# First loads in another order, conversion steps and a fourth of a convolution on GpSimd, and the last rests' y in a buffer of its own

## The chip, the cores and the metric

The kernel runs on one core of a Trainium2 chip. The metric is the device time of one execution in microseconds. TensorE (PE in the profile) multiplies matrices, VectorE (DVE), ScalarE (ACT) and GpSimd (POOL) work element by element, and SyncE (SP) issues every DMA of this kernel, in order. An instruction waits for others through semaphores, and each engine runs its own instructions in the order in which they stand.

## The reference, cut to what matters

```python
# 8 batches, 8 heads, 576 tokens, head_dim 64
kv  = einsum('bhsd,bhse->bhde', k, v)
out = einsum('bhsd,bhde->bhse', q, kv)
x   = out / sqrt(mean(out*out, -1) + 1e-6) * g_norm   # then [B, 576, 512]

gate_pre = sum(conv_w[j] * xp[:, j:j + 576, :] for j in range(5))   # xp: 4 zeros ahead
x = (sigmoid(gate_pre) * (x @ w_val)) @ w_out

h = gelu(x @ w_in); u, v = h[..., :512], h[..., 512:]
v = (v - mean(v)) / sqrt(var(v) + 1e-6) * g_ln
v = einsum('ts,bsd->btd', w_sg, v) + b_sg[None, :, None]
out = x + (u * v) @ w_out2
```

The weights w_val, conv_w, w_out, w_in and w_out2 come as 64-bit floats, the rest as 32-bit floats.

## The kernel before, in words

The work has two phases. Phase one takes the eight batches one after the other: attention (`kv`, then `o`, then a norm over each head, then a transpose `xT`), a convolution of five taps along the tokens for the gate, and two products (`val` with w_val, `y` with w_out). Its result `y_main` goes to DRAM; the last 64 tokens of four batches at a time are collected as "rests" and go to `y_rest`. Phase two reads both back and does the second block (`hv`, `hu`, `sg`, `out`).

A 32-bit product is made of three passes of TensorE: each factor is split into a high part h (rounded) and a low part l = value - h, and h*h, l*h and h*l are added up. For w_val and w_out the split starts from 64-bit floats. It is done in four pieces of 128 columns for each weight (`wv_pieces`, `wo_pieces`); `split` gives the steps of a piece, each on a tile of 128x512: ScalarE takes the magnitude (L117), VectorE does five steps (L127, L128, L120, L129, L124), ScalarE writes h (L162), and then come the last two steps, `a - h` (L167) and `l = (a - h) + c` (L169). In the kernel before, `first_weight` calls `split` with `on_pool` False: both last steps run on VectorE. `in_turn` interleaves the steps of the pieces that it is given.

The start of the program, up to the first batch's gate and the second weight's second piece, stands in a `manual_schedule` block: each engine runs these instructions in the order in which the code issues them. After that block a scheduler sets the order. Batch 0 is laid out there like this:

- the loads on SP; the conversions; `busy(n)` issues n small matmuls on a constant tile, whose result is not used, between the attention products;
- `kv_out` on ScalarE copies the attention's inner product into a block-diagonal tile `kvbd`, eight small copies, and `o` of the five token tiles reads it and Q;
- for each token tile, `square` (ScalarE), a sum (VectorE, L278), a power of -1/2 (GpSimd, L280), `scale` (VectorE, L283), a transpose (TensorE, L298), and the two parts of x (`X0h` on ScalarE, `X0l` on VectorE, L307);
- the gate: `taps` (ScalarE, L326) writes gate = tap 0 of each of the four channel blocks m, `conv` (VectorE, L332) adds taps 1 to 4 as one scalar_tensor_tensor of 128x576 for each block and tap, so 16 in all, and `sigmoid` (ScalarE) follows;
- TensorE meanwhile runs `val` of m = 0 and 1, the inner product `kv` of batch 1, and `val` of m = 2 and 3;
- `gated` (L360) multiplies each val block by its gate on VectorE, and `low` (L364) makes its low part. Only then come `o` and the norm of batch 1, whose transposes TensorE needs next.

TensorE's results stand in PSUM, in eight buffers that `bank` hands out in turn; a buffer is free again when the last reader of its earlier content is done. The scheduler has put the fifth `o` tile of batch 1 behind the VectorE read that frees a `val` buffer.

At the end, batch 7's `wout2` adds `out` to `res`, which holds `y_main`. The rests of batches 4 to 7 are added to another `res`, a tile of the same tag "Y", loaded from `y_rest` after the main part.

Of the kernel before, what the change touches and what calls it, by code (L numbers as in the profile page):

```python
# [21 lines left out]
NK = D // P  # L22
# [38 lines left out]
def body(ctx, tc, qT, k, v, gcol, w_val, conv_w, w_out, w_in, g_ln, w_sgT, b_sg, w_out2, out, out_r):  # L61
# [68 lines left out]

    def split(src, h, l, raw=None, tmp=None, k=None, on_pool=True):

# [23 lines left out]
        def steps():  # L156

            ops = st["steps"][1]
            yield ops[0]()
            yield ops[1]()  # L160
            a = ops[2]()
            act(h, flat(a), AF.Copy)  # L162
            yield
            yield ops[3]()
            c = ops[4]()
            yield
            (nc.gpsimd.tensor_tensor if on_pool else tt)(flat(a), flat(a), f32(h), op=ALU.subtract)  # L167
            yield
            tt(l, flat(a), flat(c), op=ALU.add)  # L169
            yield  # L170
# [48 lines left out]
    class Attention:  # L219
# [108 lines left out]
        def conv(self, ms):  # L328

            for j in range(1, KC):  # L330
                for m in ms:
                    stt(gate[:, m], x32[:, m, j:j + S], cw3[:, m, j:j + 1], gate[:, m], op0=ALU.mult, op1=ALU.add)  # L332

        def sigmoid(self, m):
# [296 lines left out]

    def first_weight(w, src, raws):
        return [split(src[:, m * P:(m + 1) * P], w[0][:, :, m * P:(m + 1) * P], w[1][:, :, m * P:(m + 1) * P],
                      raws[m], first[1][:, m % 2], NK, False)
                for m in range(NK)]

    wv_pieces = first_weight((wv[:, 0], wv[:, 1]), w_val, [first[0][:, i] for i in range(4)])
    wo_pieces = first_weight(wo, w_out, [spare[:, 0], spare[:, 1], first[0][:, 0], first[0][:, 1]])
    att = Attention(0)
# [17 lines left out]
    def in_turn(*pieces):  # L657

        for p in pieces:
            p[2]()  # L660
        running = [p[3]() for p in pieces]
# [4 lines left out]
    with tc.manual_schedule():  # L666
        for m in range(NK):
            wv_pieces[m][0]()
        wo_pieces[0][0]()
        att.load_kv()  # L670
        dma(gcol_s, gcol)
        dma(gln_s, g_ln)
        cw_work = taps()
        att.load_q()
        atts[1].load_kv()
        wo_pieces[1][0]()
        atts[1].load_q()
        in_turn(wv_pieces[0], wv_pieces[1])
        in_turn(wv_pieces[2], wv_pieces[3])
        wo_pieces[2][0]()  # L680
        wo_pieces[3][0]()
        busy(40)
        att.kv(0)
        busy(5)
        att.kv(1)
        busy(4)
        in_turn(wo_pieces[0])
        slots.drain()
        cw_work()
        steps = [att.o(t, None) for t in range(5)]  # L690
# [16 lines left out]
        moe = Moe(att.xh, att.xl, gate, y_main[0])  # L707
        steps[4][2]()
        for m in range(NK):
            att.taps(m)  # L710
        z = [moe.val(m, True) for m in (0, 1)]
        atts[1].kv(0)
        atts[1].kv(1)
        slots.drain()
        z += [moe.val(m, True) for m in (2, 3)]
        for a in (0, 2):
            att.conv((a, a + 1))
            att.sigmoid(a)
            att.sigmoid(a + 1)
        for m in range(NK):  # L720
            z[m][0]()
        for m in range(NK):
            z[m][1](False)
        in_turn(wo_pieces[1])
    marks = [latest()]
# [92 lines left out]
    for b in range(B):  # L818
# [23 lines left out]
        for m in range(NK):  # L842
            dma(res[:, m], y_main[b][:, m])
        if more:
            nrem = Rests((b + 1) // 2) if b % 2 else None
# [20 lines left out]
        if b % RG == RG - 1:  # L866
            res = sb("Y", [NK, RW])
            dma(res, y_rest[b // RG])
            for m in range(NK):
                wout2(m, ggr, res, out_r[b // RG])  # L870
                tick()
# [43 lines left out]
```

## Time and profile before

| what | value |
|---|---|
| time, median of 3 runs | 751.49 us (749.42 to 751.64) |
| the profiled execution: its own time, and its span | 752.53 us, 750.8 us |
| TensorE busy | 730.6 us, 97% of the span |
| VectorE busy | 589.0 us, 78% |
| ScalarE busy | 348.5 us, 46% |
| GpSimd busy | 152.1 us, 20% |

The span is the time from the first instruction to the last in the profiled execution; 1.73 us of its own time lie around it. A busy share is the part of the span in which the engine had an instruction in work. Shares of the whole say little about the first 100 us and the last 10, where the change is.

### The profile page before, as it was taken

The page shows a single profiled execution, that of the slowest core. Times are in us where ns is not written, and L with a number is a line of the kernel's source. Part 1 is how long each engine was busy: PE and PEld are TensorE (multiplying, and loading weights), DVE is VectorE, ACT ScalarE, POOL GpSimd, SP SyncE. Part 2 cuts the span into 40 slices and gives each one's busy share as a digit, 9 for nine tenths or more (in the row PEclk, how much of TensorE's full clock was granted, in tenths as well). Part 3 has the DMA queues.
Part 4 walks back from the last instruction along what each step waited for, and adds up shares of the span by engine and source line. Part 5 has one row for each costly group of instructions (what it writes and reads, how often), then busy time and mean ns, then how long its engine had stood idle before and what let it go on. Part 6 is the DMA issues. An engine that isn't in the chain of part 4 may idle for free.

```text
span 750.8 us, 11758 instructions
## 1 busy us (share of the span) xinstructions
PE 730.6 (97%) x4498; PEld 628.4 (84%) x4498; DVE 589.0 (78%) x1137; ACT 348.5 (46%) x662; POOL 152.1 (20%) x163
## 2 busy tenths in 40 slices
PE   7898999999899999999999999999999999999996
PEld 7787778778778787889989889888899888898896
DVE  6899979898779899889986786866866867867752
ACT  3657465565545756565543433434433424334320
POOL 0405437263344452221100010000100000100000
PEclk9899999999999999999999999999999999999999
DMA  9945243626144311344122211231330222111203
GB/s 284 337 138 190 86 161 134 202 87 211 56 131 158 107 69 71 106 156 142 58 70 85 71 57 56 71 99 42 99 127 10 75 85 63 64 57 43 99 1 112
DMA packets 56200, 80.15 MB, mean 107 GB/s; under 512 B 3664, under 2 KB 29264, under 8 KB 55120
## 3 DMA queue, kind: packets, MB, share of 16 engines
q1 hardware_dynamic: 56144, 79.40, 32.1%
q8 instruction: 35, 0.57, 0.3%
q14 instruction: 21, 0.17, 0.1%
HBM read 60.51 MB, written 18.87 MB: 106 GB/s over the span
## 4 chain that ended last, share of the span: by engine, by line
PE 82%; DVE 9%; DMA 3%; POOL 2%; issue 1%; ACT 1%; SPq 1%; DVEq 0%; POOLq 0%
PE sg L560 16%; PE hv L451 13%; PE out L201 12%; PE hu L201 12%; PE val L201 10%; PE y L201 9%; DVE G L332 5%; PE kv L252 3%; PE o L268 3%; PE xT L298 2%; POOL st L280 2%; PE hur L201 2%; DMA Q<-in_qT_dram 1%; DMA V<-in_v_dram 1%; DVE st L278 1%
## 5 line engine op out<-in xcount | busy, mean ns | idle before, releaser
L332 DVE SCALAR_TENSOR_TENSOR G<-X,cw,G 128x576 f32<-128x576 f32 x128 | 99.0, 819 | 6.4 <-ACT G L326 6.4
L201 PE MATMUL y<-Z,WOh 128*128 128x512 f32 (+1 forms) x320 | 100.5, 384 | 0.0
L463 POOL TENSOR_TENSOR bmv<-bmv,mhalf 128x1 f32<-128x1 f32 x36 | 21.5, 597 | 345.1 <-DVE bmv L462 345.1
L451 PE MATMUL hv<-wiv,X1h 128*128 128x512 f32 x256 | 83.3, 390 | 0.0
L201 PE MATMUL out<-Z,K 128*128 128x512 f32 x256 | 83.1, 389 | 0.0
L280 POOL TENSOR_TENSOR st<-st,mhalf 128x8 f32<-128x8 f32 (+1 forms) x40 | 74.2, 1862 | 27.4 <-DVE st L279 24.9
L201 PE MATMUL hu<-X1h,wiu 128*128 128x512 f32 x256 | 79.4, 391 | 0.0
L201 PEld LDWEIGHTS y<-Z,WOh 128*128 128x128 f32 x320 | 58.2, 189 | 11.3
L440 ACT ACTIVATE T<-T 128x512 f32<-128x512 f32 x68 | 42.9, 630 | 45.0 <-DVE T L437 44.8
L201 PE MATMUL y<-Z,WOl 128*128 128x512 f32 (+1 forms) x160 | 59.4, 373 | 0.0
L201 PEld LDWEIGHTS out<-Z,K 128*128 128x128 f32 x256 | 48.1, 188 | 10.0
L451 PEld LDWEIGHTS hv<-wiv,X1h 128*128 128x128 f32 x256 | 47.8, 188 | 9.8 <-ACT X1h L428 0.4
L201 PEld LDWEIGHTS hu<-X1h,wiu 128*128 128x128 f32 x256 | 46.6, 188 | 8.3
L561 DVE SCALAR_TENSOR_TENSOR T<-sg,gln,WOl 128x288 f32<-128x288 f32 x64 | 32.7, 516 | 26.5 <-PE sg L560 26.2
L201 PE MATMUL hu<-X1l,wiu 128*128 128x512 f32 x128 | 50.0, 391 | 0.0
L451 PE MATMUL hv<-wiv,X1l 128*128 128x512 f32 x128 | 49.9, 390 | 0.0
L201 PE MATMUL out<-Z,V 128*128 128x512 f32 x128 | 49.8, 389 | 0.0
L572 ACT ACTIVATE Z<-T 128x512 fp32r<-128x512 f32 x32 | 20.1, 631 | 58.1 <-DVE T L571 58.1
L268 PEld LDWEIGHTS o<-kvbd,Q 128*128 128x128 f32 (+1 forms) x320 | 41.0, 188 | 6.5 <-ACT kvbd L261 1.8
L268 PE MATMUL o<-kvbd,Q 128*128 128x128 f32 (+1 forms) x320 | 43.1, 283 | 1.6 <-DMA Q<-in_qT_dram 1.6
L201 PE MATMUL val<-X0h,WV 128*128 128x512 f32 x128 | 42.3, 412 | 0.0
L201 PE MATMUL val<-X1h,WV 128*128 128x512 f32 x128 | 41.3, 403 | 0.5 <-DVE T L360 0.5
(152 smaller groups left out, 1709.0 us busy)
## 6 DMA issues: line engine op xcount, KB each, us to landing
Q<-in_qT_dram SPq DMA_DIRECT2D x8, 1152.0 KB, 6.3
y_main<-Y SPq DMA_DIRECT2D x8, 1024.0 KB, 3.9
raw<-y_main SPq DMA_DIRECT2D x32, 256.0 KB, 3.1
Y<-y_main SPq DMA_DIRECT2D x32, 256.0 KB, 4.1
out_dram<-Y SPq DMA_DIRECT2D x32, 256.0 KB, 2.3
K<-in_k_dram SPq DMA_DIRECT2D x7, 1024.0 KB, 5.9
V<-in_v_dram SPq DMA_DIRECT2D x7, 1024.0 KB, 9.2
raw<-in_w_in_dram SPq DMA_DIRECT2D x16, 256.0 KB, 5.7
```

Of the source, the lines that this page charges most:

```text
L201: nc.tensor.matmul(ps, lhsT=a[:, kt, msl], rhs=x[:, kt], start=(i == 0), stop=(i == 3 * NK - 1))
L252: nc.tensor.matmul(self.pk[j][h, h], lhsT=self.k[:n, t, js][:, h], rhs=self.v[:n, t, js][:, h], start=(t == 0), stop=(t == 4))
L268: nc.tensor.matmul(po[:n, j * P:(j + 1) * P], lhsT=self.q[:, j, o:o + n], rhs=bd[:, j, :], start=True, stop=True)
L280: nc.gpsimd.tensor_tensor(st[:n, 2], st[:n, 1], mhalf[:n], op=ALU.pow)
L298: nc.tensor.transpose(pt[:, j * P:j * P + n], xo[:n, j * P:(j + 1) * P], ident[:n, :n])
L332: stt(gate[:, m], x32[:, m, j:j + S], cw3[:, m, j:j + 1], gate[:, m], op0=ALU.mult, op1=ALU.add)
L440: act(w, w, AF.Tanh, scale=CG * AG)
L451: nc.tensor.matmul(ps, lhsT=a[:, kt], rhs=p2["wiv"][:, w, kt], start=(i == 0), stop=(i == 3 * NK - 1))
L463: nc.gpsimd.tensor_tensor(mv[:, 3:4], mv[:, 2:3], mhalf[:, 0:1], op=ALU.pow)
L560: nc.tensor.matmul(ps, lhsT=a[:, msl], rhs=w, start=(n == 0), stop=(n == len(mm) - 1))
L561: later(0, lambda: stt(vs[:, sl], ps, gln_s[:, m:m + 1], p2["bsg"][:, sl], op0=ALU.mult, op1=ALU.add))
L572: act(g[:, 0], x, AF.Copy)
```

## The change

Four things change. (1) The order of the first loads, and how many dummy matmuls stand where: w_val's fourth piece is loaded after batch 0's k and v, and w_out's first piece after Q. (2) `on_pool` becomes a number: with 1 or 2 the step `a - h` runs on GpSimd, with 2 the last step too. w_val's four pieces and w_out's first two have 2, the others 1. Two more temporary tiles (in tag "Z") let the pieces run without sharing, and w_out's first two pieces are converted later: inside the first gate. (3) The gate of channel block 3 of batch 0 leaves `conv`: `conv_apart` lets ScalarE scale the shifted x and GpSimd add it to the gate, tap by tap. The low parts of `val` blocks 0 and 2 go to GpSimd too. (4) For the last batch, `y_rest` is loaded into the tag "XR", early, and not into "Y" at the end.

```diff
-    def split(src, h, l, raw=None, tmp=None, k=None, on_pool=True):
+    def split(src, h, l, raw=None, tmp=None, k=None, on_pool=1):
...
             (nc.gpsimd.tensor_tensor if on_pool else tt)(flat(a), flat(a), f32(h), op=ALU.subtract)
             yield
-            tt(l, flat(a), flat(c), op=ALU.add)
+            (nc.gpsimd.tensor_tensor if on_pool > 1 else tt)(l, flat(a), flat(c), op=ALU.add)
             yield
...
+        def conv_apart(self, m, x):
+
+            for j in range(1, KC):
+                act(x[:, j - 1], x32[:, m, j:j + S], AF.Copy, scale=cw3[:, m, j:j + 1])
+                nc.gpsimd.tensor_tensor(gate[:, m], gate[:, m], x[:, j - 1], op=ALU.add)
+
...
-    def first_weight(w, src, raws):
+    def first_weight(w, src, raws, tmps, on_pool):
         return [split(src[:, m * P:(m + 1) * P], w[0][:, :, m * P:(m + 1) * P], w[1][:, :, m * P:(m + 1) * P],
-                      raws[m], first[1][:, m % 2], NK, False)
+                      raws[m], tmps[m], NK, on_pool[m])
                 for m in range(NK)]
 
-    wv_pieces = first_weight((wv[:, 0], wv[:, 1]), w_val, [first[0][:, i] for i in range(4)])
-    wo_pieces = first_weight(wo, w_out, [spare[:, 0], spare[:, 1], first[0][:, 0], first[0][:, 1]])
+    more = sb("Z", [2, 3, D])
+    tmps = [t[:, i] for t in (first[1], more) for i in range(2)]
+    wv_pieces = first_weight((wv[:, 0], wv[:, 1]), w_val, [first[0][:, i] for i in range(4)], tmps, (2, 2, 2, 2))
+    wo_pieces = first_weight(wo, w_out, [spare[:, 0], spare[:, 1], first[0][:, 0], first[0][:, 1]],
+                             tmps[:2] * 2, (2, 2, 1, 1))
...
-        for m in range(NK):
+        for m in range(3):
             wv_pieces[m][0]()
-        wo_pieces[0][0]()
         att.load_kv()
         dma(gcol_s, gcol)
+        cw_work = taps()
+        wv_pieces[3][0]()
+        att.load_q()
+        wo_pieces[0][0]()
+        atts[1].load_kv()
         dma(gln_s, g_ln)
-        cw_work = taps()
-        att.load_q()
-        atts[1].load_kv()
         wo_pieces[1][0]()
         atts[1].load_q()
+        for m in range(3):
+            wv_pieces[m][2]()
         in_turn(wv_pieces[0], wv_pieces[1])
-        in_turn(wv_pieces[2], wv_pieces[3])
+        in_turn(wv_pieces[2])
+        cw_work()
+        wv_pieces[3][2]()
+        in_turn(wv_pieces[3])
         wo_pieces[2][0]()
         wo_pieces[3][0]()
-        busy(40)
+        busy(32)
         att.kv(0)
-        busy(5)
+        busy(12)
         att.kv(1)
-        busy(4)
-        in_turn(wo_pieces[0])
+        busy(20)
         slots.drain()
-        cw_work()
...
         steps[4][2]()
+        wo_pieces[0][2]()
         for m in range(NK):
             att.taps(m)
+        wo_pieces[1][2]()
+        in_turn(wo_pieces[0])
+        att.conv_apart(3, sb("Z", [KC - 1, S]))
         z = [moe.val(m, True) for m in (0, 1)]
...
-        for a in (0, 2):
-            att.conv((a, a + 1))
-            att.sigmoid(a)
-            att.sigmoid(a + 1)
+        att.conv((0, 1, 2))
+        for m in range(NK):
+            att.sigmoid(m)
+        in_turn(wo_pieces[1])
         for m in range(NK):
             z[m][0]()
         for m in range(NK):
-            z[m][1](False)
-        in_turn(wo_pieces[1])
+            z[m][1]()
...
+        if not more:
+            res_r = sb("XR", [NK, RW])
+            dma(res_r, y_rest[b // RG])
...
         if b % RG == RG - 1:
-            res = sb("Y", [NK, RW])
-            dma(res, y_rest[b // RG])
+            if more:
+                res_r = sb("Y", [NK, RW])
+                dma(res_r, y_rest[b // RG])
             for m in range(NK):
-                wout2(m, ggr, res, out_r[b // RG])
+                wout2(m, ggr, res_r, out_r[b // RG])
                 tick()
```

What this makes of each engine's row of instructions is shown at three places. The first is SP's first loads (`wiu` and `Y` hold the raw weights, `raw` the raw taps), before:

```order
L148 DMA wiu_88<-in_w_val_dram 128x4x256 x4
L148 DMA Y_90<-in_w_out_dram 128x4x256
L229 DMA K_102<-in_k_dram 128x2x512
L229 DMA V_103<-in_v_dram 128x2x512
L229 DMA K_102<-in_k_dram 128x2x512
L229 DMA V_103<-in_v_dram 128x2x512
L231 DMA K_102<-in_k_dram 64x512
L231 DMA V_103<-in_v_dram 64x512
L671 DMA gcol_76<-in_gcol_dram 128x1
L672 DMA gln_77<-in_g_ln_dram 128x4
L647 DMA raw_112<-in_conv_w_dram 128x40
L235 DMA Q_114<-in_qT_dram 128x4x576
```

and after the change:

```order
L150 DMA wiu_88<-in_w_val_dram 128x4x256 x3
L231 DMA K_101<-in_k_dram 128x2x512
L231 DMA V_102<-in_v_dram 128x2x512
L231 DMA K_101<-in_k_dram 128x2x512
L231 DMA V_102<-in_v_dram 128x2x512
L233 DMA K_101<-in_k_dram 64x512
L233 DMA V_102<-in_v_dram 64x512
L679 DMA gcol_76<-in_gcol_dram 128x1
L658 DMA raw_110<-in_conv_w_dram 128x40
L150 DMA wiu_88<-in_w_val_dram 128x4x256
L237 DMA Q_113<-in_qT_dram 128x4x576
L150 DMA Y_90<-in_w_out_dram 128x4x256
```

Half a megabyte of w_val and half a megabyte of w_out stood ahead of k and v; the first now stands behind them, the second behind Q.

The second is GpSimd from the end of its constants to the norm of batch 1, before (`st` with `mhalf` is the power, five for each batch):

```order
L207 MEMSET X_11_82 128x4x4
L280 TENSOR_TENSOR st_286<-st_286,mhalf_70 128x8
L280 TENSOR_TENSOR st_294<-st_294,mhalf_70 128x8
L280 TENSOR_TENSOR st_302<-st_302,mhalf_70 128x8
L280 TENSOR_TENSOR st_310<-st_310,mhalf_70 128x8
L280 TENSOR_TENSOR st_318<-st_318,mhalf_70 64x8
L279 TENSOR_SCALAR st_554<-st_554 128x8
L280 TENSOR_TENSOR st_554<-st_554,mhalf_70 128x8
```

and after the change, first the stretch up to the first power and then that from the last power of batch 0:

```order
L209 MEMSET X_11_82 128x4x4
L169 TENSOR_TENSOR wiv_89<-wiv_89,WV_79 128x512 x2
L171 TENSOR_TENSOR WV_79<-wiv_89 128x4x128 x2
L169 TENSOR_TENSOR Z_91<-Z_91,WV_79 128x512
L171 TENSOR_TENSOR WV_79<-Z_91 128x4x128
L169 TENSOR_TENSOR Z_91<-Z_91,WV_79 128x512
L171 TENSOR_TENSOR WV_79<-Z_91 128x4x128
L282 TENSOR_TENSOR st_293<-st_293,mhalf_70 128x8
```

```order
L282 TENSOR_TENSOR st_325<-st_325,mhalf_70 64x8
L169 TENSOR_TENSOR wiv_89<-wiv_89,WOh_80 128x512
L171 TENSOR_TENSOR WOl_81<-wiv_89 128x4x128
L340 TENSOR_TENSOR G_83<-G_83,Z_416 128x576 x4
L169 TENSOR_TENSOR wiv_89<-wiv_89,WOh_80 128x512
L171 TENSOR_TENSOR WOl_81<-wiv_89 128x4x128
L372 TENSOR_TENSOR Z_425<-T_439,Z_425 128x512
L281 TENSOR_SCALAR st_575<-st_575 128x8
L372 TENSOR_TENSOR Z_425<-T_510,Z_425 128x512
L281 TENSOR_SCALAR st_582<-st_582 128x8
L282 TENSOR_TENSOR st_575<-st_575,mhalf_70 128x8
```

Eight steps of w_val (names `WV`) now stand ahead of the first power, and w_out's four (`WOh`, `WOl`), the four additions of `conv_apart` (`G`) and two low parts of the gated val (`Z<-T,Z`) ahead of the first power of batch 1 (the last row).

The third is VectorE from the last low part of x, `X0l`, to the first gated val, `T<-val`, before:

```order
L307 SCALAR_TENSOR_TENSOR X0l_92<-xT_378,gcol_76,X0h_91 128x4x128
L332 SCALAR_TENSOR_TENSOR G_83<-X_11_82,cw_78,G_83 128x576 x4
L322 TENSOR_TENSOR XR_606<-X_11_82,XR_606 128x4x64
L332 SCALAR_TENSOR_TENSOR G_83<-X_11_82,cw_78,G_83 128x576 x12
L360 TENSOR_TENSOR T_413<-val_400,G_83 128x512
L360 TENSOR_TENSOR T_427<-val_414,G_83 128x512
```

and after the change:

```order
L309 SCALAR_TENSOR_TENSOR X0l_93<-xT_385,gcol_76,X0h_92 128x4x128
L127 TENSOR_SCALAR wiv_89<-Y_90 128x512
L128 TENSOR_SCALAR wiv_89<-wiv_89 128x512
L120 SCALAR_TENSOR_TENSOR wiv_89<-wiv_89 128x512
L129 TENSOR_SCALAR wiv_89<-wiv_89 128x512
L124 SCALAR_TENSOR_TENSOR wiv_89<-Y_90,wiv_89 128x512
L334 SCALAR_TENSOR_TENSOR G_83<-X_11_82,cw_78,G_83 128x576 x4
L324 TENSOR_TENSOR XR_627<-X_11_82,XR_627 128x4x64
L334 SCALAR_TENSOR_TENSOR G_83<-X_11_82,cw_78,G_83 128x576 x8
L127 TENSOR_SCALAR wiv_89<-Y_90 128x512
L128 TENSOR_SCALAR wiv_89<-wiv_89 128x512
L120 SCALAR_TENSOR_TENSOR wiv_89<-wiv_89 128x512
```

Four of the 16 conv steps are gone from VectorE, and the five steps of w_out's first piece stand ahead of the conv, those of its second piece behind it, with the first `T<-val` right after these.

## Rows read from the trace of the kernel before

**Rows 1.** Waits of TensorE (PE), 0 to 110 us; columns: us in total, times, longest

```profile
PE xT L298 <- DVE T L283: 3.2, 4, 1.2
...
PE val L201 <- DVE T L360: 0.5, 1, 0.5
```

**Rows 2.** TensorE's timeline, 2 to 30 us

```profile
2.27 11.23 PE L217 MATMUL warm<-ident 128*128 128x128 f32 x80 [2.27 <-POOL X L207]
...
23.45 6.55 PE L268 MATMUL o<-kvbd,Q 128*128 128x128 f32 x40 [1.57 <-DMA Q<-in_qT_dram]
```

**Rows 3.** Windows of 1 us on TensorE

```profile
22.00:23.00 1.00, 0.00 (x0) 0.50 0.95 344
27.00:28.00 1.00, 1.00 (x10) 0.98 1.05 401
```

**Rows 4.** VectorE's (DVE) timeline, 4 to 21 us

```profile
9.19 0.76 DVE L129 TENSOR_SCALAR wiv<-wiv 128x512 int32<-128x512 int32 x2
9.87 1.29 DVE L124 SCALAR_TENSOR_TENSOR wiv<-wiu,wiv 128x512 f32<-128x512 uint32 x2
11.07 1.28 DVE L167 TENSOR_TENSOR wiv<-wiv,WV 128x512 f32<-128x512 f32 x2
```

**Rows 5.** Groups of VectorE, 0 to 110 us; after the bars busy us and mean ns

```profile
L653 DVE TENSOR_TENSOR cw<-cv 128x20 f32<-128x20 f32 x1 | 0.2, 180 | 0.0
```

**Rows 6.** One line's instructions, all runs of it; min/median/max ns

```profile
L364 POOL TENSOR_TENSOR Z<-T,Z x18: 731/1298/1727, 96.1 to 330.2; 128x512 fp32r<-128x512 f32 x14, 128x256 fp32r<-128x256 f32 x4
```

**Rows 7.** The timeline of all engines, 303.9 to 305.6 us

```profile
303.71 1.35 POOL L364 TENSOR_TENSOR Z<-T,Z 128x512 fp32r<-128x512 f32 x1 [0.43 <-ACT Z L361]
...
304.42 1.25 DVE L332 SCALAR_TENSOR_TENSOR G<-X,cw,G 128x576 f32<-128x576 f32 x1
```

**Rows 8.** The timeline of all engines, 97.5 to 99.6 us

```profile
96.97 0.98 DVE L364 TENSOR_TENSOR Z<-T,Z 128x512 fp32r<-128x512 f32 x1
...
97.37 1.73 POOL L364 TENSOR_TENSOR Z<-T,Z 128x512 fp32r<-128x512 f32 x1
```

**Rows 9.** ScalarE's (ACT) timeline, 8 to 28 us

```profile
8.71 1.23 ACT L162 ACTIVATE WV<-wiv 128x512 fp32r<-128x512 f32 x2 [1.09 <-DVE wiv L120]
...
23.99 0.22 ACT L261 ACTIVATE kvbd<-kv 64x64 f32<-64x64 f32 x1
...
25.53 0.60 ACT L275 ACTIVATE T<-o 128x512 f32<-128x512 f32 x1 [1.08 <-PE o L268]
```

**Rows 10.** GpSimd's (POOL) timeline, 24 to 36 us

```profile
27.21 8.08 POOL L280 TENSOR_TENSOR st<-st,mhalf 128x8 f32<-128x8 f32 x5 [24.93 <-DVE st L279]
```

**Rows 11.** VectorE's timeline, 36.5 to 53.5 us

```profile
36.85 0.75 DVE L307 SCALAR_TENSOR_TENSOR X0l<-xT,gcol,X0h 128x512 fp32r<-128x512 f32 x1 [0.18 <-ACT X L303]
...
40.99 0.42 DVE L322 TENSOR_TENSOR XR<-X,XR 128x256 fp32r<-128x256 f32 x1
41.33 8.84 DVE L332 SCALAR_TENSOR_TENSOR G<-X,cw,G 128x576 f32<-128x576 f32 x12
50.08 1.88 DVE L360 TENSOR_TENSOR T<-val,G 128x512 f32<-128x512 f32 x3
52.46 0.69 DVE L360 TENSOR_TENSOR T<-val,G 128x512 f32<-128x512 f32 x1 [0.51 <-PE val L201]
```

**Rows 12.** The timeline of all engines, 56.6 to 61.2 us

```profile
56.68 3.62 PE L252 MATMUL kv<-V,K 128*64 128x64 f32 x79
...
57.28 1.64 POOL L280 TENSOR_TENSOR st<-st,mhalf 128x8 f32<-128x8 f32 x1
...
60.87 0.52 PE L298 MATMUL xT<-ident,T 128*128 128x128 f32 x3 [0.57 <-DVE T L283]
```

**Rows 13.** The timeline of all engines, from 744.5 us

```profile
744.39 0.28 PE L201 MATMUL out<-WOh,K 128*128 128x256 f32 x1
745.62 1.42 DVE L586 SCALAR_TENSOR_TENSOR Y<-out,Y 128x256 f32<-128x256 f32 x4 [5.90 <-DMA Y<-y_rest]
746.07 1.79 SPq L587 DMA_DIRECT2D out_dram<-Y  x4
```

More of the change, by code (lines that the diff above doesn't have):

```diff
@@ L657, in in_turn @@
     def in_turn(*pieces):
-        for p in pieces:
-            p[2]()
         running = [p[3]() for p in pieces]
```

## The prediction

> **What bounds the kernel now.** TensorE is the bound nearly everywhere, so I looked first for the places where it stands still, in its waits over the first 110 us. The reader is to see that little can be won there: four transposes of x wait 3.2 us in all for VectorE's scaled tiles, and one val product waits 0.5 us for a gated val of the batch before [rows 1]. Ahead of it stands the start: TensorE fills the time with 40 dummy matmuls (80 instructions, 0.281 us for two), then waits 1.57 us for Q, and the `o` products take 6.55 us [rows 2], because the granted clock is 0.50, which is 1.2 GHz, at 22 us, where TensorE has nothing to run, and back at 0.98 only in the microsecond from 27 [rows 3]. The end is the third place: the last matmul is over at 744.67, yet VectorE's last four additions start at 745.62, since the rests' y lands only then [rows 13].
>
> So the change can win at most the start, about 4 us of waits, and about 2 us of tail. What it can lose depends on what VectorE and GpSimd do to each other, which is the view I read longest.
>
> **Prices.** VectorE: a tensor_scalar of 128x512 0.34 us (two from 9.19 to 9.87), one with two inputs in SBUF 0.60 (two from 9.87 to 11.07) [rows 4]; so the five first steps of a piece 3 x 0.34 + 2 x 0.60 = 2.22, and the two last, which are moved, 1.20. A conv step 8.84 / 12 = 0.737, the step XR 0.34 [rows 11]. Six steps of the taps 6 x 0.18 = 1.1 [rows 5]. GpSimd: 1.30 for 128x512 with two inputs, 0.73 for 128x256 [rows 6]. It never ran 128x576 in this form; from the two widths 1.30 + 64 x 0.57 / 256 = 1.44, an estimate.
>
> A moved step thus takes twice as long, which would be free if GpSimd worked beside VectorE. The rows say it doesn't. A GpSimd operation ran from 303.71 to 305.06; the conv step that VectorE began at 304.42 took 1.25 us and ended at 305.67, 0.61 behind GpSimd's end [rows 7]. Turned round, VectorE's low part ended at 97.95, and the GpSimd operation that had begun at 97.37 took 1.73 us and ended at 99.10, 1.15 later [rows 8]. One waits for the other and then runs nearly its whole length: of 0.737 us 0.12 are saved, of 1.30 us 0.15, so 0.27 for each GpSimd operation set between two of VectorE's. Operations that read PSUM on VectorE were not held up.
>
> **The Trainium skill** says in "SBUF — State Buffer", section "Who interferes with whom", that a VectorE instruction with two SBUF inputs and a GpSimd instruction that reads SBUF exclude each other for a whole instruction. By the page alone, with nothing saved at a handover, the two sums below would each be 1.6 us longer and the forecast 757.4; the rows' 0.27 us is taken instead.
>
> **Step 1, the start.** At 9.33 (8.71 and half of 1.23) the first h is there [rows 9] and GpSimd wants to subtract; VectorE comes free at 9.87 [rows 4]. Until ScalarE can write the fourth piece's h, VectorE has to do two steps of the first pieces (1.20), the third piece (2.22), the taps (1.1) and three steps of the fourth (0.34 + 0.34 + 0.60 = 1.28): 5.8. GpSimd does six steps in turn with it: 7.8, less 6 x 0.27 = 1.6. That gives 9.87 + 5.8 + 7.8 - 1.6 = 21.9. Then h, 0.62, and the eight copies into kvbd, which ended at 24.21 before [rows 9] and take 1.8: 24.3. They stand behind this h on ScalarE, and TensorE's `o` waits for them. The loads are no later than that: half a megabyte less stands ahead of Q, which landed at about 23.4 [rows 2]. With 64 dummy matmuls instead of 49 TensorE has hardly stood still until then, so I take the full clock. The first `square` then comes at about 24.6, not 25.53, and the five powers, which follow one another (8.08 us for five [rows 10]), are **0.9 us earlier**. Ends: 1.6 earlier, if GpSimd takes nothing from VectorE and only the wait for Q of 1.57 [rows 2] goes; 0.7 later with no saving at handovers.
>
> **Step 2, the first gate.** I count on the clock of before and subtract 0.9 at the end. VectorE's last X0l ends at 37.60 [rows 11]. Until the conv's last step it then needs five steps of w_out's first piece (2.22), twelve conv steps (8.84) and XR (0.34); GpSimd, in turn with it, w_out's two last steps (2.60) and four additions (5.76). Six handovers save 1.6. 37.60 + 2.22 + 8.84 + 0.34 + 8.36 - 1.6 = 55.8, where the conv ended at 50.2 before [rows 11]. Who goes first hardly matters: the fourth gated val needs the last addition too. Then w_out's second piece, 2.22, stands in front of the first gated val: 58.0, not 50.08, and the fourth is done at 60.4, not 53.15 [rows 11]. TensorE has `kv` of the next batch to run until 60.3 [rows 12], but the fifth `o` tile ahead of it needs the PSUM buffer that the first gated val frees.
>
> Behind this VectorE sums the squares at once, since half of the low parts have gone. But GpSimd has four operations ahead of batch 1's first power: w_out's second piece and two low parts, 5.2 us from about 58.0, when ScalarE has written the piece's h, with half a microsecond of waits: 63.7, not 57.28 [rows 12], 6.4 later. Less the 0.9 of step 1, the first transpose of batch 1, which waited 0.57 us before [rows 12], comes 5.5 us later. The later powers find their sums ready; I take 1 us of it as made good over five tiles. TensorE is **4.5 us later**, step 1 in it. Bounds: if the additions find gaps, the three microseconds of transpose waits go away instead; without savings at handovers it is 3.3 more.
>
> **Step 3, later.** VectorE is rid of w_out's second piece (3.4) and two more steps (1.2) between 56 and 76 us, so the val wait [rows 1] goes: **0.5 less**. ScalarE's four more passes stand ahead of sigmoids that wait for VectorE's conv anyway; if the conv were done first, they would cost four times about 0.6. From there to the end TensorE is packed and keeps what it has.
>
> **Step 4, the tail.** TensorE's end plus 0.04 plus an addition of 0.42 gives 745.13 for the last addition instead of 747.04; the four issues no longer queue (1.79 us for four), and 2.94 us lie behind the last: 748.5 instead of 750.8, **2.3 less** (1.9 if the queueing stays) [rows 13]. The early load of half a megabyte follows four others on SP and waits for nothing that is late.
>
> **Step 5, the clock.** Between about 56 and 66 us TensorE now stands still twice for some microseconds. At the start it stood still in such a way, and its clock was at half for the five microseconds from 22 [rows 3]. Products at that speed cost up to 3 us; part is hidden in the waits. I take **1.0 more**, between 0 and 3.
>
> **Sum.** 4.5 - 0.5 - 2.3 + 1.0 = +2.7 us. The profiled execution took 752.53, which gives 755.2; it stood 1.0 above the median of the runs, 751.49, so I give 754.2.
>
> **Rivals.**
> - *GpSimd fits in beside VectorE* (the other side): its operations fall where VectorE reads PSUM or idles, or VectorE keeps its pace. For it speaks that VectorE stood waiting at the start and that ten microseconds of work leave it. Against it, rows 7 and 8, and a conv that leaves no gap from 38 to 50 us. Then step 1 gives 1.6, the transposes 3.2, the val 0.5, the tail 2.3: 7.6 less, 743.9; half of that, 747.7, if only the conv collides lightly. It decides at a first gated val at about 52 instead of 57.
> - *Mostly hidden* (no change): the same exclusion, but the powers run closer together and step 1 gives its full 1.6, so that TensorE is 1.8 us later and the tail and the val wait pay for it: 751.5 with half a microsecond for the clock. For it speaks that TensorE's transposes have y products between them; against it, that the first of them has none.
> - *Heavier*: nothing saved at handovers, or a clock that stays low for longer than at the start: 757 to 759.
>
> **Chances.** Forecast 0.35, heavier 0.12, mostly hidden 0.23, GpSimd beside VectorE 0.30. Within 0.3% (749.2 to 753.7, about what a measurement of this kernel tells from no change) fall the hidden case and a little of the forecast's lower end: 0.25. Faster 0.30, slower 0.45. The forecast's own range is 752 to 757; to hold eight in ten it must take in most of the fast case and the heavier one: 744.5 to 759.
>
> **What would show it.** In the profile of after: conv steps of 128x576 with a mean near 1.2 us instead of 0.81 while GpSimd adds to G; the first gated val near 57 and batch 1's first power near 63; TensorE waiting for the fifth `o` tile and the first transpose; the rests' additions at the end each following their matmuls within 0.1 us, with no load in front. The forecast is wrong if the conv steps keep 0.8 us and the transposes of batch 1 no longer wait; then the time is under 748.

## The result and the profile after

The changed kernel takes 756.68 us (median of 4 runs, 755.60 to 756.81), the kernel before 750.64 (4 runs): a ratio of 1.0076, with an interval of 1.0056 to 1.0095. It is slower by 6 us. The profiled execution shows only half of that, 755.6 beside 752.53, so a second execution of each kernel was profiled later (the last two experiments). Their landmarks stand side by side here, in microseconds from the start of each trace (starts, where no end is named; a transpose is that of one token tile):

| landmark | before, 1st | before, 2nd | after, 1st | after, 2nd |
|---|---|---|---|---|
| first `square` | 25.53 | 24.16 | 23.89 | 24.03 |
| last X0l ends | 37.60 | 35.96 | 35.61 | 35.74 |
| last conv step ends | 50.16 | 48.71 | 54.21 | 54.33 |
| first gated val | 50.08 | 48.63 | 56.71 | 56.83 |
| first power of batch 1 | 57.28 | 57.18 | 63.18 | 63.27 |
| first transpose of batch 1 | 60.87 | 60.77 | 66.92 | 67.01 |
| second transpose | 62.67 | 62.58 | 69.75 | 69.83 |
| first `y` product | 63.06 | 62.96 | 70.48 | 70.57 |
| third transpose | 65.93 | 65.83 | 74.32 | 75.43 |
| third block of `y` | 71.10 | 71.00 | 78.48 | 79.58 |
| first `hv` product | 318.66 | 318.71 | 324.19 | 326.89 |
| last matmul ends | 744.66 | 744.77 | 750.12 | 753.17 |
| span | 750.8 | 750.8 | 753.8 | 756.9 |
| own time | 752.53 | 752.56 | 755.60 | 758.64 |

First the waits of TensorE over the first 110 us (us in total, times, longest), which answer to [rows 1].

```profile
PE xT L300 <- ACT WOh L164: 5.0, 1, 5.0
PE o L270 <- DVE T L368: 3.5, 1, 3.5
PE xT L300 <- DVE T L285: 2.7, 2, 1.7
```

The val wait is gone, and two long stops have come: the fifth `o` tile waits 3.5 us for the first gated val, and the first transpose of batch 1 waits 5. The latter is put down to ScalarE's WOh, which ended at 66.84, but the scaled tile that the transpose reads was ready only at 66.78 (it starts at 66.10 and takes 0.68), so without ScalarE the wait would have been 0.1 shorter.

Next VectorE's timeline from 38 to 59 us, and GpSimd's from 40 to 70, which answer to [rows 11] and [rows 12].

```profile
38.24 4.04 DVE L334 SCALAR_TENSOR_TENSOR G<-X,cw,G 128x576 f32<-128x576 f32 x4
42.19 1.49 DVE L324 TENSOR_TENSOR XR<-X,XR 128x256 fp32r<-128x256 f32 x1
43.61 10.60 DVE L334 SCALAR_TENSOR_TENSOR G<-X,cw,G 128x576 f32<-128x576 f32 x8
54.13 0.41 DVE L127 TENSOR_SCALAR wiv<-Y 128x512 int32<-128x512 int32 x1
...
56.71 2.48 DVE L368 TENSOR_TENSOR T<-val,G 128x512 f32<-128x512 f32 x4
```

```profile
40.08 1.57 POOL L169 TENSOR_TENSOR wiv<-wiv,WOh 128x512 f32<-128x512 f32 x1 [6.50 <-ACT WOh L164]
41.73 1.68 POOL L171 TENSOR_TENSOR WOl<-wiv 128x512 fp32r<-128x512 f32 x1
43.36 7.31 POOL L340 TENSOR_TENSOR G<-G,Z 128x576 f32<-128x576 f32 x4
56.35 1.57 POOL L169 TENSOR_TENSOR wiv<-wiv,WOh 128x512 f32<-128x512 f32 x1 [5.68 <-ACT WOh L164]
58.00 1.29 POOL L171 TENSOR_TENSOR WOl<-wiv 128x512 fp32r<-128x512 f32 x1
59.25 1.29 POOL L372 TENSOR_TENSOR Z<-T,Z 128x512 fp32r<-128x512 f32 x1
60.62 0.52 POOL L281 TENSOR_SCALAR st<-st 128x8 f32<-128x8 f32 x1
61.22 1.27 POOL L372 TENSOR_TENSOR Z<-T,Z 128x512 fp32r<-128x512 f32 x1
62.58 0.52 POOL L281 TENSOR_SCALAR st<-st 128x8 f32<-128x8 f32 x1
63.18 1.71 POOL L282 TENSOR_TENSOR st<-st,mhalf 128x8 f32<-128x8 f32 x1
64.97 1.27 POOL L281 TENSOR_SCALAR st<-st 128x8 f32<-128x8 f32 x1
66.31 4.16 POOL L282 TENSOR_TENSOR st<-st,mhalf 128x8 f32<-128x8 f32 x2
```

From 40 to 51 us the two engines alternate strictly: twelve conv steps were left to VectorE, and with XR they took 15.97 us (38.24 to 54.21), where sixteen and XR took 12.09 before (38.07 to 50.16). The steps one by one, as the group of this tile gives them (min/median/max ns; first and last start):

```profile
L334 DVE SCALAR_TENSOR_TENSOR G<-X,cw,G x12: 805/810/1984, 38.2 to 53.4; 128x576 f32<-128x576 f32 x12
L340 POOL TENSOR_TENSOR G<-G,Z x4: 1591/1825/1830, 43.4 to 48.8; 128x576 f32<-128x576 f32 x4
```

The seven steps outside GpSimd's work took 0.81, the five beside it 1.85 to 1.98. Behind the conv come w_out's second piece, the gated vals, and then GpSimd's four operations, with the sums' small steps held up among them, before the first power at 63.18.

The tail, VectorE's last additions and the last matmul, answers to [rows 13]:

```profile
747.32 0.42 DVE L594 SCALAR_TENSOR_TENSOR XR<-out,XR 128x256 f32<-128x256 f32 x1 [0.99 <-PE out L203]
...
749.84 0.28 PE L203 MATMUL out<-WOh,K 128*128 128x256 f32 x1
750.15 0.42 DVE L594 SCALAR_TENSOR_TENSOR XR<-out,XR 128x256 f32<-128x256 f32 x1 [0.99 <-PE out L203]
```

Each addition follows its matmul, with no load in front. From the last matmul to the end of the span it is 3.7 us, where it was 6.1.

### The profile page after: what moved, and what is told of

It reads as the page before. It is cut to its first block, busy times and chain, and to the rows that moved or that the text cites. A ratio compares the mean times of both kernels' runs of the same rounds, so it can differ in the third digit from the quotient of the medians.

```text
span 753.8 us, 11833 instructions
## 1 busy us (share of the span) xinstructions
PE 732.5 (97%) x4528; PEld 630.2 (84%) x4528; DVE 592.0 (79%) x1117; ACT 350.8 (47%) x666; POOL 182.4 (24%) x183
## 4 chain that ended last, share of the span: by engine, by line
PE 86%; DVE 9%; POOL 3%; ACT 2%; issue 1%; POOLq 0%; DVEq 0%; ACTq 0%
PE sg L568 16%; PE hv L459 13%; PE out L203 13%; PE hu L203 12%; PE y L203 11%; PE val L203 10%; DVE G L334 6%; PE kv L254 3%; PE o L270 3%; PE warm L219 2%; PE xT L300 2%; POOL st L282 2%; PE hur L203 2%; DVE T L285 1%; DVE st L280 0%
## 5 line engine op out<-in xcount | busy, mean ns | idle before, releaser
L334 DVE SCALAR_TENSOR_TENSOR G<-X,cw,G 128x576 f32<-128x576 f32 x124 | 102.3, 871 | 5.1 <-ACT G L328 5.0
L282 POOL TENSOR_TENSOR st<-st,mhalf 128x8 f32<-128x8 f32 (+1 forms) x40 | 72.1, 1808 | 3.3 <-DVE st L281 0.9
```

The source lines that it names most:

```text
L282: nc.gpsimd.tensor_tensor(st[:n, 2], st[:n, 1], mhalf[:n], op=ALU.pow)
```

## The experiments

Times are medians; the kernel before had 750.80, 750.82 and 750.79 on the chips of the three sets. Differences "to the changed kernel" are to its 756.68.

**1. The conv alone undone.** The changed kernel with all four channel blocks of the first conv on VectorE.

```diff
-        att.conv_apart(3, sb("Z", [KC - 1, S]))
...
-        att.conv((0, 1, 2))
-        for m in range(NK):
-            att.sigmoid(m)
+        for a in (0, 2):
+            att.conv((a, a + 1))
+            att.sigmoid(a)
+            att.sigmoid(a + 1)
```

> Channel block 3 of the first gate goes back to VectorE; all else is as in the changed kernel. Theory (VectorE and GpSimd take turns): VectorE runs four more steps (4 x 0.73 = 2.9 us) but is no longer held up by the four additions (4 x 1.15 = 4.6), so the conv ends about 1.6 us earlier (52.6, not 54.2), the first gated val comes at about 55, batch 1's first power at about 61.5, and the time is about 1.6 less, 755. Rival (the additions are a relief to VectorE, and the loss sits elsewhere): 2.9 us more, about 759.5. Second rival (the conv is hidden, the queue ahead of the first power decides): the same time, 756.7.

Measured: 753.70, 3.0 less than the changed kernel; ratio to before 1.0039 (1.0027 to 1.0051). The conv ended at 52.44, the first gated val came at 54.95, the first power at 61.63: each within 0.2 of the expected. The group of this tile:

```profile
L334 DVE SCALAR_TENSOR_TENSOR G<-X,cw,G x16: 804/805/1851, 38.3 to 51.6; 128x576 f32<-128x576 f32 x16
```

Sixteen steps end 1.8 us sooner than twelve with GpSimd's help; only the two beside w_out's last steps are long (1.85 and 1.82). The time fell by more than the gate, because the first `y` came 3.1 us earlier (67.40): the fifth `o` tile no longer waited, and the second scaled tile stood 1.60 us behind the first instead of 2.81. The rival that the additions relieve VectorE is out.

**2. The conv alone, in the kernel before.** The reverse of the edit above, and nothing else of the change.

> The kernel before, with one part of the change alone: channel block 3 of the first gate on GpSimd. Theory (turns): VectorE loses four conv steps (2.9 us) and is held up four times for 1.15 (4.6): the conv ends 1.7 us later, near 51.9, and the time is 1 to 2 us more, 752 to 753. Rival (a relief): the conv ends up to 2.9 us earlier and the time falls by 1 to 3, as the transposes of batch 1 stop waiting. Second rival (hidden): the same time.

Measured: 754.26, 3.4 more than before; ratio 1.0042 (1.0028 to 1.0056). The conv ended at 50.36, 1.65 later than in the second trace of before, whose start is the same to 0.2 us. That is the price of the turns, as expected, but the time is above the expected 752 to 753. The timeline shows one thing that was not expected:

```profile
48.09 2.27 DVE L332 SCALAR_TENSOR_TENSOR G<-X,cw,G 128x576 f32<-128x576 f32 x3
52.21 2.48 DVE L366 TENSOR_TENSOR T<-val,G 128x512 f32<-128x512 f32 x4 [1.85 <-ACT G L341]
```

With three blocks interleaved all of them end together, and their sigmoids come only then, behind the rests' gate and two kvbd copies on ScalarE; VectorE waits 1.85 us. In the changed kernel w_out's second piece fills that hole, so the 3.4 is not all the price of the turns. The execution that was profiled was the fastest of the eight (752.31): its third block of `y` starts at 72.89, 1.9 late, but its clock didn't fall at 194 us as it did in both traces of before, and its last matmul ends at 744.51, not late at all. How the 3.4 of the medians divides, no trace shows.

**3. w_out's second piece behind the low parts again.** `in_turn(wo_pieces[1])` goes from ahead of the gated vals to behind the `low` calls, else as changed.

> w_out's second piece goes back behind the low parts, so that it no longer stands in front of the gated vals on VectorE; all else is as in the changed kernel. Theory (turns, and GpSimd's queue ahead of the first power): the gated vals come 2.7 us earlier, the wait for the fifth o tile falls from 3.7 to about 1, but GpSimd can only start on the piece when VectorE has done its steps, so the first power stays near 63 and the time within 0.5 of 756.7. Rival (the place of the piece is the cause): 2.7 less, 754.0.

Measured: 755.42, 1.3 less; ratio 1.0062 (1.0050 to 1.0074), which overlaps that of the changed kernel. The wait for the fifth `o` tile fell to 1.0, as expected. The first power came at 61.72, not unchanged, since the scheduler then put the sums of batch 1 between the piece's steps. Most of that was given back: the third block of `y` started at 78.15, where it was 78.48. So neither the theory's "no gain" nor the rival's full 2.7; the place of the piece is worth 0.3 by that landmark and 1.3 by the medians, whose intervals overlap.

**4. w_out's last steps on VectorE.**

```diff
-                             tmps[:2] * 2, (2, 2, 1, 1))
+                             tmps[:2] * 2, (0, 0, 1, 1))
```

> The last two steps of w_out's first two pieces go back to VectorE; order and all else as in the changed kernel. Theory: in the conv two turns of GpSimd go (2 x 1.15) and 1.2 us of VectorE come, 1.1 less; w_out's second piece costs VectorE 1.2 more in front of the gated vals, so these come at the same time as in the changed kernel; GpSimd has only two low parts left ahead of the first power, which comes near 61 instead of 63.2: 2 us less, 754.7. Rival (GpSimd's steps relieve VectorE): 2.4 us more, 759.

Measured: 756.55, the same as the changed kernel; ratio 1.0085 (1.0072 to 1.0098). The expectation failed, and VectorE's timeline shows why:

```profile
37.83 0.69 DVE L124 SCALAR_TENSOR_TENSOR wiv<-Y,wiv 128x512 f32<-128x512 uint32 x1
39.71 0.43 DVE L324 TENSOR_TENSOR XR<-X,XR 128x256 fp32r<-128x256 f32 x1 [1.19 <-ACT XR L323]
40.23 0.69 DVE L169 TENSOR_TENSOR wiv<-wiv,WOh 128x512 f32<-128x512 f32 x1
```

On ScalarE the piece's h stands behind the four taps, so VectorE waited 1.2 us for it. The first gated val came at 59.01, 2.3 later. GpSimd's queue ahead of the first power did get short, but what stood ahead of the queue had become longer.

**5. The whole first gate back on VectorE.** Edits 1, 3 and 4 together, and `low(False)`; start and tail stay as changed, and w_out's first piece stays in front of the conv.

> The new order of the start and the tail of the changed kernel stay; the first gate is as in the kernel before (all four blocks, the low parts and w_out's first two pieces on VectorE, the second piece behind the low parts), but the first piece stands in front of the conv. Theory (everything lost is lost in the first gate): first gated val near 51.5, first power near 58.7, TensorE 0.5 to 1.5 us later than in the kernel before at batch 1 and the tail 2.4 us shorter: 749 to 750.5. Rival (the start's order costs something later, or the lower clock comes anyway): 753 or more.

Measured: 752.48, 4.2 less than the changed kernel; ratio 1.0026 (1.0017 to 1.0035). The first power was back at 57.34, but the conv started 5.7 us behind the last X0l (0.5 in experiment 7), with the same wait on ScalarE in between, and TensorE's clock was 0.63 and 0.52 in the windows from 60 and from 64 us. The gate holds most of the loss. The time is 2.0 to 3.5 us more than expected and close to the rival's 753. Beside the trace of experiment 7 the first power is 1.2 us late, which is what w_out's first piece between X0l and the conv leaves there; the first `y` (64.42) is 2.5 late and its third block (73.67) 3.7, so the larger part arises behind the power, in the order of batch 1 and at the lower clock. The run doesn't separate these.

**6. The start undone.** The changed kernel with the order of loads of before, its dummy matmuls (40, 5, 4), and w_val's pieces on VectorE.

> The changed kernel with the start of the kernel before: its order of loads, its numbers of dummy matmuls, w_val's pieces on VectorE; w_out's first piece, the gate and the tail stay as changed. Theory (the start is worth half a microsecond, since in four traces of kernels with the old start the first square came at 24.1 to 25.5, 24.6 in the mean, and in five with the new one at 23.9 to 24.4; and a lower clock at the start may add up to 1.3): 757.2 to 758.5. Rival (the start is what costs, since the kernel with the new start, the new tail and the old gate is 1.7 slower than before and the tail gives back 3): 753 to 754.

Measured: 757.63, 0.95 more than the changed kernel; ratio 1.0093 (1.0071 to 1.0115), and the two intervals overlap. Its first `square` came at 23.73 and its last X0l ended at 35.52, as early as in the changed kernel. So this part of the start is no loss, and its gain is between nothing and a microsecond. It is not the whole start of the kernel before: w_out's first piece stays in the gate, and without it the eight copies into kvbd begin at 19.72 on ScalarE, where they began at 22.36 and 21.23 in the two traces of before. What the start gains by the piece's leaving it was not tried alone.

**7. The tail alone, in the kernel before.**

```diff
+        if not more:
+            res_r = sb("XR", [NK, RW])
+            dma(res_r, y_rest[b // RG])
...
-            res = sb("Y", [NK, RW])
-            dma(res, y_rest[b // RG])
+            if more:
+                res_r = sb("Y", [NK, RW])
+                dma(res_r, y_rest[b // RG])
```

> The kernel before, with one part of the change alone: the last rests' y in the tag XR, loaded early. Theory: the last addition follows the last matmul by half a microsecond instead of 2.4; 2.4 us less than the kernel before, 748.4. Rival (the early load stands in the way of another, or the stores at the end queue): within 1 us of the kernel before.

Measured: 747.70, 3.1 less than before; ratio 0.9954 (0.9937 to 0.9971). It is faster than both kernels. The last matmul and the last addition:

```profile
743.33 0.28 PE L201 MATMUL out<-WOh,K 128*128 128x256 f32 x1
743.65 0.42 DVE L586 SCALAR_TENSOR_TENSOR XR<-out,XR 128x256 f32<-128x256 f32 x1 [0.99 <-PE out L201]
```

The span ends at 746.9, 3.3 us behind the last matmul, which is 2.8 less than before. This trace is also 1.1 us ahead of both traces of before at the last matmul, and as much at the first power (56.17), where the edit changes nothing: its clock fell in the windows from 20 and 24 us (0.81 and 0.77) and held at 36.

**8. An attempt to keep the start's gain.** As experiment 5, but w_out's first piece is loaded ahead of Q, five of its steps stand ahead of the norms and the last two between them, all on VectorE.

> The start and the tail of the changed kernel, and the first gate as before, all on VectorE; w_out's first piece is loaded ahead of Q and converted on VectorE in the hole that the changed start leaves there from 22 us, its last two steps between the norms. Theory (the start's gain is real, and all that was lost was lost in the first gate): conv from about 36 to 48.5, first gated val near 48.5, batch 1's first power near 56, TensorE 1.5 to 2 us ahead of the kernel before, the tail 2.4 shorter: 746.5. Rival (Q or the first powers come a microsecond later, and the gain of the start is gone): 748.4, as with the tail alone. Second rival (TensorE stops longer ahead of batch 1 and its clock falls): 748 to 750.

Measured: 752.14; ratio 1.0015 (1.0006 to 1.0024). The attempt failed. VectorE's and GpSimd's timelines at that place:

```profile
22.41 1.49 DVE L127 TENSOR_SCALAR wiv<-Y 128x512 int32<-128x512 int32 x1
23.82 1.49 DVE L128 TENSOR_SCALAR wiv<-wiv 128x512 f32<-128x512 f32 x1
25.34 0.69 DVE L120 SCALAR_TENSOR_TENSOR wiv<-wiv 128x512 int32<-128x512 int32 x1
```

```profile
22.05 1.56 POOL L169 TENSOR_TENSOR Z<-Z,WV 128x512 f32<-128x512 f32 x1 [2.60 <-ACT WV L164]
23.69 1.33 POOL L171 TENSOR_TENSOR WV<-Z 128x512 fp32r<-128x512 f32 x1
```

The hole was none: GpSimd worked in it, on w_val's fourth piece, and VectorE's first two steps took 1.49 each instead of 0.42. The piece's h then came at 26.07, in front of the squares on ScalarE, the first of which started at 26.72 instead of 23.89.

**9. The dummy matmuls alone.** Experiment 7 with `busy` 32, 12, 20 in place of 40, 5, 4.

> The kernel before with the new tail and the changed kernel's numbers of dummy matmuls (32, 12, 20), nothing else of the start. Theory (the old start lets TensorE stand still, and its clock falls either at 22 to 27 us or at 36 to 40): the clock stays at 1.00 up to 40 us, and the time is 0.5 to 1.3 less than with the tail alone, 746.4 to 747.2. Rival (VectorE's gate is the later one anyway): the same, 747.7. Second rival (the dummy matmuls stand in front of o): up to 1 more.

Measured: 751.60, 3.9 more than with the tail alone; ratio 1.0013 (1.0002 to 1.0025). The clock did stay at 1.00 up to 40 us. But a new wait came, in TensorE's timeline:

```profile
70.07 1.05 PE L268 MATMUL o<-kvbd,Q 128*128 128x128 f32 x8
73.25 0.50 PE L201 MATMUL y<-Z,WOl 128*128 128x512 f32 x1 [2.12 <-DVE WOl L169]
```

and on VectorE:

```profile
72.52 0.67 DVE L169 TENSOR_TENSOR WOl<-wiv 128x512 fp32r<-128x512 f32 x1
```

The number of dummy matmuls is known to the scheduler, and it put batch 1 in another order. The first product of `y` with the low part of w_out's third piece now follows 8 products of `o`; in experiment 7, 24 of `o` and the first of val stand ahead of it, so that it starts only at 75.82. The piece's last step itself comes at 72.52, not 71.37, and `y` waits 2.1 us for it. By the two traces the kernel is 2.05 us later at its last matmul; the rest of the 3.9 isn't shown. The edit doesn't isolate the clock, and what the clock is worth there stays open. The same holds for every edit inside the hand-ordered block: the order behind it moves too.

**10 and 11. Both kernels once more**, for a second trace each.

> The kernel before once more, for a second trace. Theory: its first trace was one of its slower executions (752.5, where the median is 750.8), because TensorE's clock fell to half at 22 to 27 us and at 194 to 198 us; in a faster one the second of these is missing. Rival: both are there in every execution, and the difference lies elsewhere.

> The changed kernel once more, for a second trace. Theory: its first trace was its fastest execution (755.6, where the median is 756.7), because TensorE's clock didn't fall at 196 to 200 us, as it did at that place in both traces of the kernel before; a slower one shows it there. Rival: it never falls there in the changed kernel.

Measured: 752.56 and 758.64. Windows of TensorE (the number behind the count is the granted clock) in the second trace of before:

```profile
20.00:24.00 4.00, 2.77 (x33) 1.00 0.81 248
36.00:38.00 2.00, 1.99 (x5) 0.60 1.08 345
194.00:198.00 4.00, 4.00 (x19) 0.65 0.20 66
```

In this one the clock held at 22 us, where it was 0.50 in the first trace [rows 3], and fell at 36 instead, in the val products. At 194 it fell in both. With the fall at 36 the earlier start won nothing: VectorE's fourth gated val waited 1.86 us for its val product (0.51 in the first trace [rows 11]), and the first power of batch 1 came as late as there, 57.18.

```profile
52.36 0.69 DVE L360 TENSOR_TENSOR T<-val,G 128x512 f32<-128x512 f32 x1 [1.86 <-PE val L201]
```

The same places in the two traces of the changed kernel, the first ahead:

```profile
68.00:72.00 4.00, 2.26 (x9) 0.50 0.66 227
72.00:76.00 4.00, 4.00 (x22) 0.93 0.01 2
...
198.00:202.00 4.00, 2.02 (x17) 1.00 0.00 0
```

```profile
68.00:72.00 4.00, 2.26 (x9) 0.50 0.98 336
72.00:76.00 4.00, 4.00 (x16) 0.64 0.04 11
...
202.00:206.00 4.00, 4.00 (x20) 0.67 0.20 66
```

Up to the first `y` the two executions of the changed kernel agree within 0.15 us (the table above). What makes 3 us between them is the clock: it came back later in the second (1.1 us at the third block of `y`), and fell again at 202, where the first kept it. That is what was expected of a slower execution of the changed kernel. The expectation on the kernel before can't be judged: this execution was no faster than the first (752.56), and two falls are there again, the first of them at another place.

## Why the forecast was right in direction and too small

The forecast was 754.2 with a range up to 759; it came out at 756.7. Slower was right, and the mechanism too, but the agreement of the sum, +2.7, with the first pair of traces, +3.07, is chance. By the second pair it is +6.1, as in the medians.

**Step 1, the start (-0.9).** h of the fourth piece came at 20.93 and the first `square` at 23.89, both earlier than worked out. But 1.4 of the 1.6 us gained on [rows 9] belong to that execution of the kernel before, whose clock was at half: its second trace has its first square at 24.16. Measured: 0.1 to 1.6 by the traces, 0.95 and not certain by experiment 6, which leaves out what w_out's first piece does there.

**Step 2, the first gate (TensorE 4.5 later, step 1 in it).** This is the term that was mis-sized most: without what the clock cost it measures 6.1 and 6.2 at the third block of `y`. Its parts up to the first power came out 0.4, 0.7 and 1.5 us longer than said. From the last X0l the conv was to end after 18.2 us and ended after 18.6; the first gated val was to come after 20.4 and came after 21.1; the first power after 26.1, and it came after 27.6. Two small steps of the sums, 0.52 us each, stood in GpSimd's queue ahead of that power, and the prediction left them out. An earlier last X0l (1.99 us in the first pair, where 0.9 was said) made up for most of it. The handover was as taken from [rows 7, 8]: the four held steps from 43.61 to 51.21 took 1.90 a turn, where 0.737 and 1.44 (the estimate) without any overlap make 2.18, so 0.28 is saved, where 0.27 was said. In "SBUF — State Buffer", section "Who interferes with whom", the Trainium skill lets the two engines exclude each other for a whole instruction; the trace agrees on the exclusion and differs on its length by these 0.28 us a turn. That its forecast, 757.4, lies nearer to the time is no evidence for it, since the missing part arose elsewhere.

Most of it arose behind the first power. How late TensorE is, in us, against the kernel before:

| at | 1st pair | 2nd pair | prediction |
|---|---|---|---|
| first transpose of batch 1 | 6.05 | 6.24 | 5.5 |
| second transpose | 7.08 | 7.25 | no term |
| third transpose | 8.39 | 9.60 | no term |
| third block of `y` | 7.38 | 8.58 | 5.5, of which 1.0 for the clock |

The first transpose is 0.6 to 0.7 later than said. The second tile adds 1.0, for which the sum had no term: its scaled form came 2.81 us behind the first, where it was 1.80 before.

```profile
66.10 0.68 DVE L285 TENSOR_TENSOR T<-o,st 128x512 f32<-128x512 f32 x1
66.70 0.67 DVE L120 SCALAR_TENSOR_TENSOR wiv<-wiv 128x512 int32<-128x512 int32 x1
68.91 0.69 DVE L285 TENSOR_TENSOR T<-o,st 128x512 f32<-128x512 f32 x1 [1.54 <-POOL st L282]
```

On GpSimd the sum's small step took 1.27 us at 64.97 and the power behind it 2.56 (the first of the two from 66.31 shown above), where the first trace of before has 0.20 to 0.34 and 1.94, while VectorE ran two-input steps of w_out's third and fourth pieces at 65.50 and 66.70. So the turns go on behind the gate, and the prediction priced them only in it. (They are there in the kernel before too, whose third power took 2.59; the rows of the two kernels differ in where they fall.) In experiment 1 the distance of the two tiles is 1.60.

Up to the third transpose the same products follow without a wait in all four traces, but at half the clock in the changed kernel, which adds 1.31 and 2.35: that is step 5's. Behind it 1.0 came back, since the changed kernel no longer waits for its fourth tile (0.79 before). So the 1 us "made good" was right, and went to pay for the second tile.

**Step 3, the val wait (-0.5).** It went. Between the third block of `y` and 120 us TensorE's lateness fell by 0.3 in both pairs (7.38 to 7.06 in the first).

**Step 4, the tail (-2.3).** 2.4 and 2.3 in the two pairs of traces, 2.8 in the trace and 3.1 in the medians of experiment 7. Right.

**Step 5, the clock (+1.0, 0 to 3).** It fell where it was said to, around the stops ahead of batch 1, and cost 1.31 us in the first pair and 2.35 in the second, inside its bounds, but 1.35 too small in the second. One reading was wrong. The half clock of [rows 3] didn't begin at 22 us with TensorE idle; the windows ahead of that one show it with dummy matmuls running:

```profile
20.00:21.00 1.00, 1.00 (x8) 0.61 1.05 397
21.00:22.00 1.00, 0.88 (x5) 0.50 1.10 273
```

What the step missed is that the clock of before is no constant either: in the first pair it fell at 194 us in the kernel before alone, and TensorE's lateness shrank there from 7.06 to 5.53. With these terms the sums close: 7.4 - 0.3 - 1.5 - 0.1 - 2.4 = 3.1 in the first pair, and 8.6 - 0.3 - 0.1 + 0.2 - 2.3 = 6.1 in the second (from the third block of `y` on: the val wait, the clock at 194, what lies up to `hv` and behind it, the tail). Of the 3.4 us that the forecast's sum lacks in the second pair, the first transpose has 0.7, the second tile 1.0 and the clock 1.35; the rest is small.

**The rivals.** "GpSimd fits in beside VectorE" falls with experiments 1 and 2: taking the additions back gains 3.0, putting them alone loses 3.4. "Mostly hidden" falls with the first `y`. "Heavier" has the time nearly right (757 to 759). Of its two reasons the first fails, since the handovers saved what was said; the second, a clock that stays low for longer, is there in the second trace (0.59 from 58 to 62 us and 0.50 from 66 to 74 by its windows), whose time of 758.64 lies in its range. The sum of "mostly hidden" gives 751.0 from its own terms (751.49 + 1.8 + 0.5 - 2.3 - 0.5), not 751.5.

**What would show it.** The conv steps' mean from 38 to 54 us was 1.28 (seven of 0.81, five of 1.85 to 1.98; near 1.2 was said), the first gated val 56.7 (near 57), the first power 63.2 (near 63), both waits were there, and the additions at the end followed their matmuls.

**What stays open.** The parts don't add up to within a microsecond: from before, the tail gives 3.1 back and the conv costs 3.0 to 3.4, so some 6 us, and whatever the start gains, are left for w_out's pieces in the gate, the low parts and the later order together. Experiment 5 points to w_out's first piece ahead of the conv (the conv starts 5.7 us behind the last X0l there, 2.6 in the changed kernel, 0.5 before), but its trace has the larger loss behind the first power. Each of experiments 3 to 5 also moved the scheduler's order, and neither the first piece nor the low parts were moved alone.

## What to carry to other kernels

Before work is moved from VectorE to GpSimd, look in the trace for one place where both run at once on SBUF, and read the length of each there; if they take turns, a moved operation costs its own length in the queue of the engine that it was to relieve, and goes on costing wherever that queue meets the other. Cost such a move up to the first instruction of the bounding engine that needs the last of the queue, not up to the end of the stage. Where a block ordered by hand is followed by a scheduler, any edit inside moves the order behind it, so compare the order before a part is charged with the difference; and where one profile stands above the median of its runs, take a second before differences of a few microseconds are explained.

## What the runs showed of the hardware that was not expected

- VectorE's operations with a single input take turns with GpSimd too: a tensor_scalar of 128x512 took 1.49 us (0.42 elsewhere) while GpSimd ran (experiment 8), and in the changed start one of 128x20 took 0.78 and two with two inputs 1.13, where 0.18 is usual. Beside GpSimd's power of 128x8 at 63.18 four of 128x512 kept their 0.42.
- Two executions of one kernel, equal to 0.15 us in every landmark of the first 71 us, ended 3.05 us apart, and the rows where they part are those of the granted clock: 0.93 in the window from 72 to 76 us in one and 0.64 in the other, and at 0.67 from 202 to 206 us in the other alone.
